# The first six items of a chunked-attention and MLP kernel: one written order of single operations for four engines

## The chip, the cores and the metric

The kernel runs on one core of one Trainium2 chip. The metric is the device time of the whole kernel in microseconds, from one execution to the next; a profile of one execution shows where it goes. Engines are named as the profile names them: PE (TensorE), DVE (VectorE), ACT (ScalarE), POOL (GpSimd), SP (SyncE, which only issues DMAs here).

## What is computed

Attention in chunks of 32 queries, each over 16 keys to the left, its own 32, 8 to the right and 8 memory keys, and behind it two layers of MLP on all 3072 tokens:

```python
# q, k, v: (4, 8, 768, 64); mem_k, mem_v: (4, 8, 8, 64)
for c in range(24):
    k_full = concat(mem_k, k[l_start:r_end])
    scores = scale * matmul(q_c, k_full.T)
    a = exp(scores - max(scores))
    a = a / (sum(a) + 1e-9)
    out[c] = matmul(a, v_full)
x = out as (3072, 512)
h = x @ w_in                       # 512 -> 2048
x = maximum(0.01 * h, h) @ w_out   # 2048 -> 512
return ((x @ w_a) * (x @ w_b)) @ w_out2
```

Matrix products are made with three matmuls each: an operand is split into a rounded high part and a low part that is the rest (xh and xl of the activations, `w[:, 0]` and `w[:, 1]` of a weight, gh and gl of a hidden block).

## The kernel before

**Attention** goes by units of 128 tokens (24 units). For a unit u the kernel loads q, two tiles of keys and two of values, and then goes through these steps: `a_scores(u)` (L273), 32 small matmuls on PE; `a_max(u)` (L293), the maximum of a row and its subtraction on VectorE; `a_exp(u)` (L306), the exponential on ScalarE; `a_soft2(u)` (L325), sum, reciprocal and product on VectorE; `a_turn_mm` (L358), four transposes on PE, and `a_turn_copy` (L369), two copies on ScalarE; `a_pv` (L381), 32 matmuls with the values on PE; `a_out` (L421), the high part on ScalarE and the low part on VectorE. For units in `by_scalar` (L291: 2 and 3) VectorE only negates the maximum, and ScalarE makes eight exponentials of a row each, which subtract and sum at once.

**The first MLP layer** goes by blocks of 512 tokens and by items f of 128 hidden columns. `mm1_pe` (L521) makes a hidden product h_f (12 matmuls), `mm1_act` (L528) its activation g, high part gh (ScalarE) and low part gl (VectorE), `mm2` (L546) the product a_f with the second weight into four accumulators. In block 0 the items 0 to 2 are half items, of the first 256 tokens alone (units 0 and 1); from item 3 on an item needs units 0 to 3.

**Weights** (`class Weights`, L131) arrive as raw 64-bit words, 512 KB a block, in the order h0, h1, h2, a0, h3, a1, h4, a2, ... (numbers 0, 1, 2, ...). A block goes through five steps: `w_bias` on ScalarE (L102), two joins on VectorE (L115, L118), a cast on ScalarE and a low part on VectorE (`cast`, `low`). `step()` (L190) takes one block a step further, twice an item. Blocks of a second weight are also written back to DRAM (`wod`) for later token blocks.

**The order.** `InOrder` (L33) wraps PE, VectorE, ScalarE and SP: as long as it is on, each engine issues in the order in which the code calls it. It is on from the first load through the lines at L458 to L511 and `first_items()` (L611), which ends it. From item 3 on (L987) the order is the scheduler's. `fill(n)` (L471) issues n idle products of the identity with itself on PE (two matmuls each in the trace). Twelve fills stand in the beginning, in two calls.

Buffers that tie steps: four key tiles and four value tiles (two units), two score banks, two p tiles, four raw buffers for the blocks of second weights, three z tiles, two PT tiles, so unit u+2's keys wait until unit u's scores have read theirs, and its values until unit u's product with values has.

Of the kernel before, what the change touches and what calls it, by code (L numbers as in the profile page):

```python
# [55 lines left out]
def kernel(  # L56
# [51 lines left out]
    def w_join(raw, z, part=None):  # L108
        lo, hi = raw[:, :, 0], raw[:, :, 1]
        if part != 1:  # L110
            w_join_hi(hi, z)
        if part != 0:
            w_join_lo(lo, z)
# [17 lines left out]
    class Weights:  # L131
# [7 lines left out]
        def load(self, upto):  # L139
            while self.loaded < min(upto, len(self.order)):  # L140
                f, i = self.order[self.loaded]
                if i:
                    raw = prep.tile([P, 512, 2], I32, tag="raw", name="raw", bufs=4)
                else:
                    raw = wp.tile([P, 512, 2], I32, tag=f"wi{f}", name="raw")
                sp.dma_start(
                    out=raw.rearrange("p n w -> p (n w)"), in_=w1_l[f, i].bitcast(I32)
                )
                self.raw[self.loaded] = raw
                self.loaded += 1  # L150

# [5 lines left out]
        def join(self, part=None):  # L157
            n = self.joined
            if part != 1:
                self.bias(n + 1)  # L160
                self.z[n] = tp.tile([P, 512], I32, tag="z", name="z", bufs=3)
            w_join(self.raw[n], self.z[n], part)
            if part != 0:
                self.raw.pop(n)
                self.joined += 1

        def cast(self, upto):
            while self.casted < min(upto, self.joined):
                n = self.casted
                f, i = self.order[n]  # L170
                pool, tag = (wop, "wo") if i else (wp, f"wi{f}")
                w = pool.tile([P, 2, 512], F32R, tag=tag, name="w")
                act.copy(w[:, 0, :], self.z[n].bitcast(F32))
                wslot[f, i] = w
                self.casted += 1

        def low(self, upto):
            self.cast(upto)
            while self.parted < min(upto, self.joined):
                f, i = self.order[self.parted]  # L180
                w = wslot[f, i]
                dve.tensor_tensor(
                    out=w[:, 1, :], in0=self.z.pop(self.parted).bitcast(F32),
                    in1=w[:, 0, :].bitcast(F32), op=ALU.subtract,
                )
                if i:
                    sp.dma_start(out=wod[f], in_=w.bitcast(F32))
                self.parted += 1

# [101 lines left out]
    by_scalar = (2, 3)  # L291

    def a_max(u):  # L293
        s = st[u]
        m = sm.tile([P, 8], F32, tag="m", name="m", bufs=2)
        dve.reduce_max(m, s, axis=AX.X)
        p = ap_.tile([P, 8, 64], F32, tag="p", name="p", bufs=2)
        if u in by_scalar:
            dve.tensor_scalar(m, m, -scale, None, ALU.mult)
        else:  # L300
            dve.tensor_tensor(
                out=p, in0=s, in1=m.unsqueeze(2).to_broadcast([P, 8, 64]), op=ALU.subtract
            )
        pt_[u] = p, m

    def a_exp(u):  # L306
        s = st.pop(u)
        p, m = pt_[u]
        if u in by_scalar:
            l = sm.tile([P, 8], F32, tag="l", name="l", bufs=2)  # L310
            for r in range(8):
                act.activation(
                    p[:, r], s[:, r], AF.Exp, bias=m[:, r:r + 1], scale=scale,
                    accum_out=l[:, r:r + 1],
                )
            sums[u] = l
        else:
            act.activation(p, p, AF.Exp, scale=scale)
        pt_[u] = p

    def a_soft1(u):
        a_max(u)
        a_exp(u)

    def a_soft2(u):  # L325
# [5 lines left out]
        if u in sums:  # L331
            l = sums.pop(u)
        else:
            l = sm.tile([P, 8], F32, tag="l", name="l", bufs=2)
            dve.reduce_sum(l, p, axis=AX.X)
# [247 lines left out]
    HALF, LEAD = TB // 2, 3  # L583
    items = []
# [25 lines left out]

    def first_items():  # L611
        parts = [items[f][2] for f in range(LEAD)]
        W1.join()
        a_soft2(2)
        h0 = mm1_pe(0, parts[0])
        g0 = mm1_act(*h0)
        W1.bias(4)
        W1.cast(3)
        W1.bias(5)
        a_scores(3)  # L620
        a_max(3)
        W1.low(3)
        a_turn_mm(2, ps_a, "a")
        a_turn_copy(2)
        a_exp(3)
        h1 = mm1_pe(0, parts[1])
        a_pv(2, ps_s, "s")
        W1.join()
        W1.join(0)
        a_soft2(3)  # L630
        W1.join(1)
        W1.cast(4)
        W1.low(4)
        a_out(2, ("x", 0), 2 * UT)
        load_qk(2)
        W1.load(12)
        load_v(2)
        W1.load(13)
        g1 = mm1_act(*h1)
        h2 = mm1_pe(0, parts[2])  # L640
        a_turn_mm(3, ps_s, "s")
        mm2(0, parts[0], g0)
        a_turn_copy(3)
        W1.cast(5)
        W1.bias(6)
        W1.low(5)
        a_pv(3, ps_s, "s")
        W1.join(0)
        a_out(3, ("x", 0), 3 * UT)
        W1.join(1)  # L650
        W1.bias(7)
        g2_low = mm1_act(*h2, low=False)
        W1.cast(6)
        W1.join(0)
        W1.low(6)
        W1.join(1)
        g2 = g2_low()
        W1.cast(7)
        W1.bias(8)
        load_qk(3)  # L660
        load_v(3)
        W1.low(7)
# [324 lines left out]
    for bi, f, parts in items[LEAD:]:  # L987
# [640 lines left out]
```

## Time and profile before

| | us |
|---|---|
| median of 3 runs (lowest, highest) | 1120.43 (1120.24, 1121.39) |
| the profiled execution, own time | 1120.36 |
| its span, first to last instruction | 1118.5 |
| PE busy in the span | 1096.0 (98%) |
| VectorE busy | 772.9 (69%) |
| ScalarE busy | 526.6 (47%) |

The share of busy time tells which engine is the bound over the whole; an idle stretch is found in the 40 slices and in the list of waits, and what stands before and behind it in the timeline. All times below are counted from the start of the span. Matmuls are pipelined: a row's duration overlaps the next, and the distance between starts is what PE takes. Names in the rows are those of the program: s scores, p probabilities, pT and pt the turned ones, pv the product with values, warm the fills, raw, z and w the weight's steps, h, g, gh, gl and a as above. In the first 41 us most lines are L49, the one where `InOrder` issues.

### The profile page before, as it was taken

The numbers are of one execution on the slowest core, as the hardware profiler recorded it, in microseconds if no ns is written. First come the engines' busy times: TensorE is split into PE (matmuls) and PEld (weight loads), VectorE is DVE, ScalarE is ACT, GpSimd is POOL, SyncE is SP. The second block draws the span as 40 slices with busy tenths as digits, with TensorE's granted clock in tenths as the row PEclk, the third lists the DMA queues.
The fourth block names the chain that finished last, engine by engine and source line by source line (L and its number), as shares of the span: only waits on it lengthen the run. The fifth ranks groups of instructions, "written<-read, shape, count | busy, mean of one in ns | idle before, by whom it ended". The sixth has DMA issues, their size and how long they took to land.

```text
span 1118.5 us, 16332 instructions
## 1 busy us (share of the span) xinstructions
PE 1096.0 (98%) x6195; PEld 908.6 (81%) x6195; DVE 772.9 (69%) x1417; ACT 526.6 (47%) x893; POOL 7.4 (1%) x18
## 2 busy tenths in 40 slices
PE   7899999999999999999999999999999999999997
PEld 6788888888888888877788888888888888888886
DVE  6796388978898665778551737588736578745676
ACT  5887556664555235666622424144434243433232
POOL 2000000000000000000000000000000000000000
PEclk9999999999999999999999999999999999999999
DMA  9996889889998423556688756566877566767452
GB/s 315 404 345 229 282 308 344 297 337 365 327 325 335 158 81 135 186 200 226 246 329 290 266 191 201 181 211 193 275 229 219 166 220 192 242 182 242 143 185 76
DMA packets 99854, 270.63 MB, mean 242 GB/s; under 512 B 9664, under 2 KB 24128, under 8 KB 99008
## 3 DMA queue, kind: packets, MB, share of 16 engines
q1 hardware_dynamic: 98032, 267.88, 70.4%
q10 hardware_dynamic: 1744, 1.70, 0.5%
q8 instruction: 49, 0.80, 0.3%
q14 instruction: 29, 0.24, 0.1%
HBM read 215.02 MB, written 54.53 MB: 241 GB/s over the span
## 4 chain that ended last, share of the span: by engine, by line
PE 81%; DVE 9%; ACT 5%; DMA 3%; issue 1%; SPq 1%; DVEq 0%; ACTq 0%
PE ca L49 18%; PE cc L49 9%; PE oa L49 9%; PE a L49 7%; PE cb L49 5%; PE oy L49 4%; PE h L438 4%; PE a L562 4%; PE a L566 3%; PE a L565 3%; PE h L439 3%; PE h L440 3%; DVE pt L351 2%; PE A L49 2%; PE oz L49 1%; PE pv L391 1%
## 5 line engine op out<-in xcount | busy, mean ns | idle before, releaser
L49 PE MATMUL ca<-ch,wab 128*128 128x512 f32 x576 | 192.2, 389 | 0.0
L49 ACT CAST st<-gb 128x512 fp32r<-128x512 f32 x126 | 76.5, 621 | 124.5 <-DVE gb L49 123.9
L49 PEld LDWEIGHTS ca<-ch,wab 128*128 128x128 f32 x576 | 108.1, 188 | 23.2 <-ACT a L49 0.4
L49 PE MATMUL ca<-cl,wab 128*128 128x512 f32 x288 | 112.2, 389 | 0.0
L49 PE MATMUL oa<-st,wt 128*128 128x512 f32 x420 | 104.3, 389 | 0.0
L438 PE MATMUL h<-xh,w 128*128 128x512 f32 (+1 forms) x256 | 100.5, 393 | 2.8 <-DVE xl L425 2.1
L49 PE MATMUL cc<-ch,wab 128*128 128x512 f32 x288 | 100.3, 389 | 0.0
L439 PE MATMUL h<-xl,w 128*128 128x512 f32 (+1 forms) x256 | 98.6, 385 | 0.2 <-DVE xl L49 0.2
L440 PE MATMUL h<-xh,w 128*128 128x512 f32 (+1 forms) x256 | 98.5, 385 | 0.0
L562 PE MATMUL a<-gh,w 128*128 128x512 f32 (+1 forms) x256 | 97.7, 382 | 0.5 <-ACT x L580 0.5
L565 PE MATMUL a<-gl,w 128*128 128x512 f32 (+1 forms) x256 | 97.5, 381 | 0.0
L566 PE MATMUL a<-gh,w 128*128 128x512 f32 (+1 forms) x256 | 97.5, 381 | 0.0
L49 DVE TENSOR_TENSOR st<-gb,st 128x512 fp32r<-128x512 f32 x126 | 85.3, 689 | 15.0 <-ACT st L49 13.3
L49 PEld LDWEIGHTS oa<-st,wt 128*128 128x128 f32 x420 | 78.8, 188 | 16.4
L49 ACT COPY u<-ca 128x512 f32<-128x512 f32 x72 | 42.3, 587 | 91.5 <-PE ca L49 91.4
L351 DVE STREAM_TRANSPOSE pt<-p 32x128 f32<-32x128 f32 x256 | 77.4, 302 | 3.5
L49 PEld LDWEIGHTS cc<-ch,wab 128*128 128x128 f32 x288 | 54.1, 188 | 11.3
L49 PEld LDWEIGHTS ca<-cl,wab 128*128 128x128 f32 x288 | 54.1, 188 | 11.1
L530 ACT ACTIVATE g<-h 128x512 f32<-128x512 f32 (+1 forms) x64 | 37.3, 583 | 54.2 <-PE h L440 53.9
L536 DVE TENSOR_TENSOR gl<-g,gh 128x512 fp32r<-128x512 f32 (+1 forms) x64 | 43.0, 672 | 26.8 <-ACT gh L533 23.2
L438 PEld LDWEIGHTS h<-xh,w 128*128 128x128 f32 x256 | 48.1, 188 | 13.3 <-DVE xl L425 2.5
L562 PEld LDWEIGHTS a<-gh,w 128*128 128x128 f32 x256 | 48.1, 188 | 10.3 <-ACT x L580 0.9
(198 smaller groups left out, 2050.7 us busy)
## 6 DMA issues: line engine op xcount, KB each, us to landing
wab<-wab SPq DMA_DIRECT2D x126, 512.0 KB, 4.4
w<-wod SPq DMA_DIRECT2D x80, 512.0 KB, 5.3
raw<-w SPq DMA_DIRECT2D x68, 512.0 KB, 7.0
wt<-wtd SPq DMA_DIRECT2D x63, 512.0 KB, 4.5
k<-kl SPq DMA_DIRECT2D x48, 256.0 KB, 4.8
v<-vl SPq DMA_DIRECT2D x48, 256.0 KB, 5.6
wab<-pwb SPq DMA_DIRECT2D x12, 768.0 KB, 5.5
wod<-w SPq DMA_DIRECT2D x16, 512.0 KB, 6.8
```

Source lines behind the costliest of these rows:

```text
L49: self.last = emit(*args, **kwargs).ins
L351: dve.transpose(out=pt[o0:o0 + 32, :, 2 * cpar + hpar, hpx, :], in_=p[i0:i0 + 32, hpx::2, 32 * b:32 * b + 32],)
L391: pe.matmul(o[64 * hpar:64 * hpar + 64, 2 * pair:2 * pair + 2, t0:t0 + CH], v[:, i:i + 64], pt[:, 2 * cp + pair, 2 * cpar + hpar].rearrang ...
L438: pe.matmul(ps, w[1], x[0], start=first, stop=False)
L439: pe.matmul(ps, w[0], x[1], start=False, stop=False)
L440: pe.matmul(ps, w[0], x[0], start=False, stop=last)
L530: act.activation(g[:, c], ps[:, c], AF.Prelu, alpha=0.01)
L536: dve.tensor_tensor(out=gl[:, c], in0=g[:, c], in1=gh[:, c].bitcast(F32), op=ALU.subtract)
L562: pe.matmul(ps, slot[:, 1, c], gh[:, t], start=f == 0 and o == 0, stop=False, **kw)
L565: pe.matmul(ps, slot[:, 0, c], gl[:, t], start=False, stop=False, **kw)
L566: pe.matmul(ps, slot[:, 0, c], gh[:, t], start=False, stop=f == NF1 - 1 or (o == HALF and f == LEAD - 1), **kw)
```

## The change

The single steps are made callable one by one (`a_sub`, `a_neg`, `a_sum`, `a_inv`, `a_mult`, `load_one`, `cast_one`, `low_one`, `store`, the two joins), and one string, `FIRST`, lists them in the order in which they are called, for all four engines. It covers the items 0 to 5: in it a word is an operation with its number (s scores, m maximum, d subtraction, n negation, e exponential, S sum, l reciprocal, p product, T turn, ca and cb its copies, O product with values, xh and xl the parts of the output, b, zh, zl, c, w the weight's steps, h, g, gh, gl, a the item's, Qa and Qb the halves of a unit's placement, F fills, q, k, v, raw, id, st DMAs).

- Keys of unit 2 and 3 and their queries are loaded ahead of values and of most weights; weight blocks come in the order 1, 2, 0, 3, 4, 12, 5, 14, 6, 9, 8, 7, 13, ...
- The second half of q and the second key tile of units 0 and 1 are issued by ScalarE's queue.
- The scores of units 0 to 3 come before the first product with values; the score of unit 4, its maximum, subtraction and exponential come within the list.
- Unit 3 leaves `by_scalar`: its subtraction and sum move to VectorE.
- Fills: 8, 5, 11 and 10 in place of 6 and 6.
- The turn of unit 3 and the products with values of units 2 and 3 use the bank pool of the accumulators.
- The fixed order ends behind item 5 (`FIXED = 6`) with 12 weight blocks done and 16 loaded; before it ended with item 2. From item 6 on the scheduler orders as before.

```diff
             if u < len(qs):
-                eng = act if u < 1 else sp
+                eng = act if u < 2 else sp
...
             t = ap_.tile([P, 512], F32, tag="k", name="k")
-            sp.dma_start(out=t, in_=ku[u][cp])
+            (act if u < 2 and cp else sp).dma_start(out=t, in_=ku[u][cp])
...
-    by_scalar = (2, 3)
+    by_scalar = (2,)
...
+    def a_sub(u):
+        p, m = pt_[u]
+        dve.tensor_tensor(
+            out=p, in0=st.pop(u), in1=m.unsqueeze(2).to_broadcast([P, 8, 64]), op=ALU.subtract
+        )
+
+    def a_neg(u):
+        m = pt_[u][1]
+        dve.tensor_scalar(m, m, -scale, None, ALU.mult)
...
-    q_load(1)
-    k_load(2)
-    q_load(2)
-    k_load(4)
-    sp.dma_start(out=ident, in_=id_l)
-    W1.load(1)
-    v_load(2)
-    W1.load(2)
-    q_load(3)
...
-    a_scores(0)
-    a_scores(1)
-    fill(6)
-    k_load(6)
-    v_load(4)
-    W1.load(3)
-    q_load(4)
-    k_load(8)
-    W1.load(5)
-    a_max(0)
-    a_exp(0)
-    W1.bias(1)
-    a_soft2(0)
-    a_turn_mm(0, ps_a, "a")
-    fill(6)
-    a_max(1)
-    a_turn_copy(0, (0,))
-    a_exp(1)
-    a_turn_copy(0, (1,))
-    W1.bias(2)
-    a_pv(0, ps_h, "h")
-    v_load(6)
-    W1.load(7)
-    W1.join(0)
-    a_soft2(1)
-    W1.join(1)
-    a_out(0, ("x", 0), 0)
-    a_turn_mm(1, ps_a, "a")
-    a_scores(2)
-    a_turn_copy(1)
-    W1.join()
-    W1.cast(2)
-    W1.low(1)
-    a_max(2)
-    a_pv(1, ps_h, "h")
-    v_load(8)
-    W1.load(11)
-    a_out(1, ("x", 0), UT)
-    W1.bias(3)
-    W1.low(2)
-    a_exp(2)
...
+    FIXED, DONE = 6, 12
...
+    FIRST = """
+        q0 k0 q1 k1 s0 q2 k2 m0 d0 s1 e0 raw1 S0 m1 s2 id l0 q3 k3 d1 p0 e1 m2 b1 T0 F8 n2 raw2
+        S1 e2 zh1 zl1 s3 v0 l1 p1 ca0 l2 cb0 raw0 T1 p2 c1 m3 T2 F5 b2 v1 d3 cb1 O0 F11 zh2 e3
+        raw3 w1 ca1 zl2 xh0 v2 S3 b0 l3 ca2 raw4 O1 F10 xl0 c2 zh0 cb2 v3 zl0 xh1 p3 c0 raw12
+        xl1 T3 b3 O2 w0 ca3 raw5 w2 h0 b4 zh3 cb3 raw14 zh4 xh2 O3 zl4 g0 raw6 zl3 gh0 h1 c4 xl2
+        raw9 xh3 w4 h2 b5 xl3 raw8 g1 zh5 c3 h3 gl0 g2 raw7 zl5 b6 w3 gh1 c5 zh6 q4 raw13 zl6 b9
+        a0 k4 w5 c6 gl1 b8 k5 w6 a1 b7 zh8 gh2 zl8 Qb4 h4 zh9 raw10 zh7 Qa4 zl7 raw15 gl2 c7 s4
+        c8 w7 raw11 g3 zl9 a2 w8 v4 c9 gh3 m4 h5 v5 b10 d4 w9 e4 st0 b11 gl3 g4 zh10 a3 st1 zh11
+        g5 zl11 st2 zl10 c11 w11 c10 gh5 w10 q5 st3 gh4 gl5 gl4 st4
+    """
...
+        op("q", lambda u: q_load(u + 1))
+        op("k", lambda u: k_load(2 * u + 2))
+        op("v", lambda u: v_load(2 * u + 2))
+        op("id", lambda n: sp.dma_start(out=ident, in_=id_l))
+        op("raw", W1.load_one)
+        op("st", lambda f: W1.store(f))
+        op("s", a_scores)
+        op("m", a_max)
+        op("d", a_sub)
+        op("n", a_neg)
+        op("e", a_exp)
+        op("S", a_sum)
+        op("l", a_inv)
+        op("p", a_mult)
+        op("T", a_turn_mm, ps_a, "a")
+        op("ca", a_turn_copy, (0,))
+        op("cb", a_turn_copy, (1,))
+        op("O", lambda u: a_pv(u, *((ps_h, "h") if u < 2 else (ps_a, "a"))))
+        op("xh", out_hi)
+        op("xl", out_lo)
+        op("b", lambda n: w_bias(W1.raw[n]))
+        op("zh", zh)
+        op("zl", zl)
+        op("c", W1.cast_one)
+        op("w", W1.low_one)
+        for name, fn in (("h", h), ("g", g), ("gh", gh), ("gl", gl), ("a", a)):
+            op(name, fn)
+        op("Qa", q_place_half, 0)
+        op("Qb", q_place_half, 1)
+        op("F", fill)
+        for word in FIRST.split():
+            name = word.rstrip("0123456789")
+            ops[name](int(word[len(name):] or 0))
+        qr.pop(4)
+        W1.loaded = 16
+        W1.biased = W1.joined = W1.casted = W1.parted = DONE
+        load_qk(4)
         for e in (pe, dve, act, sp):
             e.on = False
-        return [(0, parts[1], g1), (0, parts[2], g2)]
-
-    at(0, 3, q_place, 4, nc.scalar.copy)
+        return [(0, items[f][2], made.pop(f)) for f in (FIXED - 2, FIXED - 1)]
...
     for k, f in enumerate([5, 8, 11, 14]):
         u = TB // UT + k
-        at(0, f, a_scores, u)
-        at(0, f, load_qk, u)
-        at(0, f, a_soft1, u)
+        if k:
+            at(0, f, a_scores, u)
+            at(0, f, load_qk, u)
+            at(0, f, a_soft1, u)
...
-    for bi, f, parts in items[LEAD:]:
+    for bi, f, parts in items[FIXED:]:
```

## Rows read from the trace of the kernel before

**Rows 1.** The page, parts 1 and 2: PE's share of the span, and 40 slices.
```profile
PE 1096.0 (98%) x6195; PEld 908.6 (81%) x6195; DVE 772.9 (69%) x1417; ACT 526.6 (47%) x893; POOL 7.4 (1%) x18
...
PE   7899999999999999999999999999999999999997
```

**Rows 2.** PE's waits, whole span: waiting <- releaser: us, times, longest.
```profile
PE s L46 <- DMA k<-kl: 6.1, 1, 6.1
PE h L438 <- DVE xl L425: 2.1, 3, 0.9
```

**Rows 3.** PE's timeline: start us, us, instruction, count; idle time and releaser.
```profile
8.56 2.04 PE L49 MATMUL s<-k,qs 128*64 128x64 f32 x32 [0.39 <-DMA k<-kl]
...
12.63 0.60 PE L49 MATMUL pT<-id,p 128*128 128x128 f32 x4
13.06 1.50 PE L49 MATMUL warm<-id 128*128 128x128 f32 x12
...
16.90 2.00 PE L49 MATMUL s<-k,qs 128*64 128x64 f32 x32
18.74 1.10 PE L49 MATMUL pv<-pt,v 128*64 128x64 f32 x32
...
26.91 1.15 PE L49 MATMUL pv<-pt,v 128*64 128x64 f32 x32
27.99 0.39 PE L49 MATMUL h<-xh,w 128*128 128x256 f32 x1
...
38.58 0.28 PE L562 MATMUL a<-gh,w 128*128 128x256 f32 x1
...
38.93 0.28 PE L562 MATMUL a<-gh,w 128*128 128x256 f32 x1
...
52.28 0.50 PE L438 MATMUL h<-xh,w 128*128 128x512 f32 x1
...
55.14 0.39 PE L562 MATMUL a<-gh,w 128*128 128x512 f32 x1
...
57.86 0.39 PE L438 MATMUL h<-xh,w 128*128 128x512 f32 x1
```

**Rows 4.** The chain of waits, 0 to 120 us: start us, us, what.
```profile
3.90 4.53 DMA k<-kl
...
21.04 2.37 ACT p L49 x16
...
70.50 0.93 PE s L282 x32
```

**Rows 5.** Stretches: length, busy us by engine, granted clock, DMA share, GB/s.
```profile
0.00:5.00 5.00, 0.00 (x0) 0.00 (x0) 0.97 (x2) 1.28 (x1) 4.25 (x12) 1.00 0.42 122
...
10.00:20.00 10.00, 9.24 (x140) 8.52 (x136) 8.70 (x18) 6.37 (x12) 0.00 (x0) 1.00 1.05 343
20.00:30.00 10.00, 8.69 (x104) 7.81 (x104) 7.33 (x19) 9.93 (x43) 0.00 (x0) 1.00 1.04 401
...
8.20:52.30 44.10, 38.88 (x417) 33.71 (x417) 36.33 (x72) 35.10 (x86) 0.00 (x0) 1.00 1.03 386
```

**Rows 6.** ScalarE's timeline: its wait for the first weight block.
```profile
11.52 0.69 ACT L49 ACTIVATE raw<-raw 128x512 f32<-128x512 f32 x1 [1.22 <-DMA raw<-w]
```

**Rows 7.** VectorE by shape, 0 to 52.3 us: count, busy us, mean ns, idle before.
```profile
L49 DVE TENSOR_TENSOR w<-z,w 128x512 fp32r<-128x512 f32 x7 | 4.8, 690 | 1.7 <-ACT w L49 1.7
...
L116 DVE TENSOR_SCALAR z<-raw 128x512 int32<-128x512 int32 x6 | 2.4, 421 | 0.0
```

**Rows 8.** ScalarE by shape, 0 to 52.3 us.
```profile
L49 ACT ACTIVATE raw<-raw 128x512 f32<-128x512 f32 x8 | 5.4, 681 | 1.2 <-DMA raw<-w 1.2
...
L49 ACT ACTIVATE p<-p 128x512 f32<-128x512 f32 x2 | 1.3, 630 | 7.0 <-DVE p L49 7.0
```

**Rows 9.** Two stretches, the fills alone (x is the count of matmuls).
```profile
10.50:11.75 1.25, 1.22 (x5) 1.22 (x6) 1.00 1.01 365
13.05:14.30 1.25, 1.24 (x12) 1.25 (x12) 1.00 1.02 267
```

More of the change, by code (lines that the diff above doesn't have):

```diff
@@ L106, in w_bias, with w_join @@
         act.activation(hi, hi, AF.Prelu, scale=2.0 ** -112, alpha=2.0 ** 32)
[L108 to L113, printed above, removed]
+    def w_join(raw, z):
+        w_join_hi(raw[:, :, 1], z)
+        w_join_lo(raw[:, :, 0], z)
     def w_join_hi(hi, z):
@@ L140, in load, with load_one @@
             while self.loaded < min(upto, len(self.order)):
[L141 to L149, printed above, removed]
-                self.loaded += 1
+                self.load_one(self.loaded)
+                self.loaded += 1
+        def load_one(self, n):
+            f, i = self.order[n]
+            if i:
+                raw = prep.tile([P, 512, 2], I32, tag="raw", name="raw", bufs=4)
+            else:
+                raw = wp.tile([P, 512, 2], I32, tag=f"wi{f}", name="raw")
+            sp.dma_start(
+                out=raw.rearrange("p n w -> p (n w)"), in_=w1_l[f, i].bitcast(I32)
+            )
+            self.raw[n] = raw
         def bias(self, upto):
@@ L179, in low, with low_one, store @@
             while self.parted < min(upto, self.joined):
+                self.low_one(self.parted)
                 f, i = self.order[self.parted]
[L181 to L185, printed above, removed]
                 if i:
-                    sp.dma_start(out=wod[f], in_=w.bitcast(F32))
+                    self.store(f)
                 self.parted += 1
+        def low_one(self, n):
+            w = wslot[self.order[n]]
+            dve.tensor_tensor(
+                out=w[:, 1, :], in0=self.z.pop(n).bitcast(F32),
+                in1=w[:, 0, :].bitcast(F32), op=ALU.subtract,
+            )
+        def store(self, f):
+            sp.dma_start(out=wod[f], in_=wslot[f, 1].bitcast(F32))
         def step(self):
@@ L290, with a_exp, a_sum @@
     pt_, sums = {}, {}
-    by_scalar = (2, 3)
+    by_scalar = (2,)
     def a_max(u):
-        s = st[u]
         m = sm.tile([P, 8], F32, tag="m", name="m", bufs=2)
[L296 to L302, printed above, removed]
-            )
[L304 to L319, printed above, removed]
+        dve.reduce_max(m, st[u], axis=AX.X)
+        pt_[u] = ap_.tile([P, 8, 64], F32, tag="p", name="p", bufs=2), m
+    def a_sub(u):
+        p, m = pt_[u]
+        dve.tensor_tensor(
+            out=p, in0=st.pop(u), in1=m.unsqueeze(2).to_broadcast([P, 8, 64]), op=ALU.subtract
+        )
+    def a_neg(u):
+        m = pt_[u][1]
+        dve.tensor_scalar(m, m, -scale, None, ALU.mult)
+    def a_exp(u):
+        p, m = pt_[u]
+        pt_[u] = p
+        if u not in by_scalar:
+            act.activation(p, p, AF.Exp, scale=scale)
+            return
+        s = st.pop(u)
+        l = sums[u] = sm.tile([P, 8], F32, tag="l", name="l", bufs=2)
+        for r in range(8):
+            act.activation(
+                p[:, r], s[:, r], AF.Exp, bias=m[:, r:r + 1], scale=scale,
+                accum_out=l[:, r:r + 1],
+            )
     def a_soft1(u):
         a_max(u)
+        a_sub(u)
         a_exp(u)
-    def a_soft2(u):
+    def a_sum(u):
         p = pt_[u]
@@ L330, in a_soft2, with a_inv, a_mult @@
             dve.memset(p[64:128, 4:8, WIN - RIGHT:WIN], 0.0)
[L331 to L335, printed above, removed]
+        l = sums[u] = sm.tile([P, 8], F32, tag="l", name="l", bufs=2)
+        dve.reduce_sum(l, p, axis=AX.X)
+    def a_inv(u):
+        l = sums[u]
         dve.tensor_scalar(l, l, 1e-9, None, ALU.add)
         dve.reciprocal(l, l)
+    def a_mult(u):
+        p, l = pt_[u], sums.pop(u)
         dve.tensor_tensor(
@@ L340, in a_soft2 @@
         )
+    def a_soft2(u):
+        a_sum(u)
+        a_inv(u)
+        a_mult(u)
     def a_turn(u):
@@ L609, in load_v @@
         v_load(2 * u + 6)
-    def first_items():
[L612 to L662, printed above, removed]
@@ new lines, with q_place_half, zh, zl @@
+    """
+    def first_items():
+        made, ops = {}, {}
+        def q_place_half(u, h):
+            t = qr[u].rearrange("p q o -> p o q")
+            d = slice(64 * h, 64 * h + 64)
+            act.copy(q_tile(u)[d, :, CH * h:CH * h + CH], t[d])
+        def zh(n):
+            W1.z[n] = tp.tile([P, 512], I32, tag="z", name="z", bufs=3)
+            w_join_hi(W1.raw[n][:, :, 1], W1.z[n])
+        def zl(n):
+            w_join_lo(W1.raw.pop(n)[:, :, 0], W1.z[n])
+        def h(f):
+            made[f] = mm1_pe(0, items[f][2])
+        def g(f):
+            ps, c = made[f]
+            t = tp.tile([P, TB], F32, tag="t", name="g")
+            act.activation(t[:, c], ps[:, c], AF.Prelu, alpha=0.01)
+            made[f] = t, c
+        def gh(f):
+            t, c = made[f]
+            x = tp.tile([P, TB], F32R, tag="gh", name="gh", bufs=3)
+            act.copy(x[:, c], t[:, c])
+            made[f] = t, c, x
+        def gl(f):
+            t, c, x = made[f]
+            y = tp.tile([P, TB], F32R, tag="gl", name="gl", bufs=3)
+            dve.tensor_tensor(
+                out=y[:, c], in0=t[:, c], in1=x[:, c].bitcast(F32), op=ALU.subtract
+            )
+            made[f] = x, y
+        def a(f):
+            mm2(0, items[f][2], made.pop(f))
+        def out_hi(u):
+            act.copy(x1["x", 0][0][:, :, u * UT:u * UT + UT], pvt[u])
+        def out_lo(u):
+            hi, lo = [t[:, :, u * UT:u * UT + UT] for t in x1["x", 0]]
+            dve.tensor_tensor(out=lo, in0=pvt.pop(u), in1=hi.bitcast(F32), op=ALU.subtract)
+        def op(name, fn, *args):
+            ops[name] = lambda n: fn(n, *args)
+        op("q", lambda u: q_load(u + 1))
[35 more added lines that the diff above has]
+        load_qk(4)
```

27 lines of the change are left out of this document (13 added, 14 removed).

## Prediction

> **What bounds the kernel now.** I read the page first: PE is busy 98% of the span, and the digits of its row are 9 from the second slice on [rows 1]. So an order of work can pay only at the beginning. The list of PE's waits says the same: the largest is the 6.1 us before the first scores, and of the later ones only the 2.1 us ahead of L438 stand out [rows 2]. Then PE's timeline: the rows to look at are the start of item 6's first product at 52.28 us and those behind it, at 55.14 and 57.86, which follow without a gap [rows 3]. From 52.28 us on PE simply works; whatever the change gives must be there by then. At that point the kernel of before has done, on PE, the hidden products h0 to h5, the output products a0 to a3, units 0 to 3 and the scores of unit 4. The fixed list of the change ends with exactly the same PE work. So the forecast is one question: **when does the changed kernel reach h6?** Each us there is a us at the end, as far as the later work follows PE, which its gapless rows say.
>
> **What PE must do in the list, piece by piece** [rows 3, 4]. Scores of a unit from the strided tiles: 16.90 to 18.74, 1.84 us. Scores of unit 4: 0.93. A turn (four transposes): 12.63 to 13.06, 0.44. A product with values: 26.91 to 27.99, 1.08. Half items: three matmuls of 256 columns take 38.58 to 38.93, so twelve take 1.43. Full items: 55.14 to 57.86, 2.73. A fill is two matmuls of 128 columns: twelve take 1.50 us with the tail of the last, and the four transposes of the same size 0.11 each; I take 0.111, so 0.223 for a fill.
> The change has F8, F5, F11 and F10: 34 fills, 7.6 us, against 12 (2.7 us) now. They stand in PE's queue and can't be skipped; this is the cost that is added on the path. What it can remove is PE's idle and stretched time: over 8.2 to 52.3 us PE is busy 38.88 of 44.10 us, fills included [rows 5].
>
> **Loads.** Their order sets when PE's list begins in earnest. Now the queue carries q0, k0, q1, k1 (1.57 MB), the identity, a weight block (2.16 MB), values, another weight block, and only then k2 and, after more of the same, k3. The first weight block has landed at 11.52 us, where ScalarE's wait for it ends [rows 6]; from there the DMA engines are full (share 1.05) and move 343 GB/s until 20 us and 401 GB/s after it [rows 5]. With keys ahead of values, k2 is complete at 2.36 MB, the identity at 2.95 and k3 at 3.74: 11.52 + 0.20/0.343 = 12.1 us, 13.8 us, and 11.52 + 1.57/0.343 = 16.1 us. Unit 2's scores now begin at 16.90 [rows 3] and could begin almost 5 us earlier.
> The ACT queue takes halves of q0, q1, k0 and k1. Before 5 us the DMA engines are used at 0.42 [rows 5], and SP reaches the key block of unit 1 only at 3.90 us, which then takes until 8.43 [rows 4]. Issuing four of eight loads elsewhere can move the stream forward by 0 to 1.1 us; I take 0, since k2 must still wait until unit 0's scores have read k0's buffers, and keep 1.1 for the early end. The Trainium skill ("DMA: Bandwidth & Descriptors", section "Issuing engines are not separate DMA queues") speaks against a gain here: starting DMAs from several engines saves only the time of starting them. By it the sum stays as it is; the low share before 5 us says that the starting does cost something in this stretch.
> The weights pay for it: the block that a2 needs becomes the last of 11.6 MB. At these rates it lands at 36.3 us; a2 comes at 43.2 us below. Its five steps (ScalarE 0.68, VectorE 0.42 and 0.69, ScalarE 0.63, VectorE 0.69) take 3.1 us [rows 7, 8], so 3.8 us are left for queueing. Off the path.
>
> **The sum.** T0 waits for the identity, 13.8 us. (Unit 0's softmax is earlier: its turn starts at 12.63 now [rows 3], and one more VectorE operation of 0.69 stands ahead of its last step that unit 0's exponential doesn't cover: 13.3.) Then in PE's order: T0 0.44 and F8 1.78 end at 16.0; k3 is there at 16.1. From there s3 1.84, T1 and T2 0.88, F5 1.11, O0 1.08, F11 2.45, O1 1.08, F10 2.23 (26.8 us); T3 0.44, O2 1.08, h0 1.43, O3 1.08, h1 and h2 2.86, h3 2.73, a0 and a1 2.86, h4 2.73, s4 0.93, a2 1.43, h5 2.73, a3 2.73: **h6 at 49.8 us** if nothing waits. The values of units 0 and 1 (4.78 and 5.83 MB: 19.2 and 21.9 us) are there before O0 (19.9) and O1 (23.6).
>
> **Who else could be late.** VectorE now works 36.33 us between 8.2 and 52.3 and idles 7.8 [rows 5]. Up to the block that h6 needs the list has four large operations more (unit 4's maximum and subtraction are earlier, unit 3 subtracts and sums on VectorE), one small one less, one weight block less and two large gl less: 4 x 0.69 - 0.17 - 1.80 - 1.38 = -0.6, so 35.7 us. That block is ready at 8.2 + 35.7 = 43.9 us plus VectorE's idle time: 5.9 us of it are free, and with the 7.8 us of now h6 would start at 51.7. ScalarE loses work: eight exponentials with sums of unit 3, 2.37 us [rows 4], become one of 0.63 [rows 8]; it is 35.10 of 44.10 us busy [rows 5] and not the bound. The methods split into single operations issue the same instructions and cost nothing; half of unit 4's placement and its exponential only move on ScalarE.
>
> **The clock.** The column of the granted clock reads 1.00, that is 2.4 GHz, from the start [rows 5], but from 10.50 us on five fill matmuls and six weight loads go in 1.25 us (0.21 each by the loads), from 13.05 on twelve of both [rows 9]: the full rate shows only after PE had worked from 6.1 us with no pause over 0.39 us [rows 2, 3]. In the list PE pauses between s1 (ends about 10) and s2 (about 12). If the full rate comes only at the end of F8, T0 and F8 take 0.87 + 16 x 0.21 and s3 starts at 18.1 instead of 16.1: h6 at 51.8. No row shows the case, so these are the two ends, 49.8 and 51.8. I take the middle, 50.8, since the pause is short and F8 alone is longer than the 1.2 us of fills before the rise now, and add 0.2 for handovers: **h6 at 51.0, 1.3 us ahead of 52.28.** The Trainium skill ("TensorE: Matmul & The Clock Gate", "Part 1: The HAM clock gate") says that the array starts at the lower rate and that the moment of the rise changes from run to run; by it neither end is ruled out, and the doubled number of fills agrees with such a rise.
>
> **Rivals.** (1) *Early.* The second queue brings the stream up to 1.1 us forward and the rate rises before F8: s3 starts at 15.0 to 15.9, h6 at 48.8 to 49.8, a gain of 2.5 to 3.5 us, 1116.9 to 1117.9. For it: DMA engines half idle before 5 us. Against: k2 waits for unit 0's scores, and VectorE may then idle under 5.9 us. (2) *VectorE becomes the bound:* it idles as much as now, h6 at 51.7, 1119.8; with one us more of it 1120.8. For it: twelve weight blocks go to and fro between ScalarE and VectorE in a fixed order, where one late operand holds all behind it. Against: four softmaxes that come earlier fill its early gaps. (3) *The clock, slower than before.* If the rate stays low past F8, the price beside the 2.0 us is 0.9 for T1 and T2, 1.1 for F5, 2.4 for F11 and 2.2 for F10. It makes the kernel slower by over 2.2 us (h6 past 54.5) from a rise at about 26 us on, in F11; low through F10 gives h6 at 58.4, 1126.5. For it: PE's pause before s2. Against: by then PE would have worked without a pause for 14 us. (4) *SP's queue stands.* The third unit's values wait for O0 and the fourth's for O1, and behind them in SP's order are five weight blocks that a1, h4, a2, h5 and a3 need. O1 ends at 24.6; a load took 4.5 us (3.90 to 8.43) [rows 4], so the stream may pause 2 us and a2's block land at 38.3, within its 3.8 us. If O1 ends 4 us later than summed, a2 waits, 1120.5 to 1123.
>
> **How the numbers follow.** The profiled execution took 1120.36 us, 1.86 more than its span of 1118.5; the median of the runs is 1120.43, so I work from 1120.36. Forecast 1120.36 - 1.3 = 1119.1 us, chance 0.50, its own range 1118.2 to 1120.5. Rival 1: 0.28. Rival 2: 0.08. Rival 3: 0.07. Rival 4: 0.07, of which 0.03 lie above the bound. A measurement of this kernel tells about 0.2%, 2.2 us, from no change. So faster 0.28, same 0.50 + 0.08 + 0.04 = 0.62, slower 0.07 + 0.03 = 0.10. The range goes from 1117.0 (rival 1 all but whole) to 1121.8 (rival 4's middle); rival 3 is left out.
>
> **What would show it.** Right: s3 at 16 to 18 us, T3 at 27 to 29, h6's first row of L438 at 50 to 52, no PE wait over 0.5 us between s2 and h6. Six fill loads to 1.25 us after 17 us would show the slow rate; VectorE idle for over 6 us with h6 waiting for a weight block rival 2; s3 before 15.9 rival 1; ScalarE waiting for a weight's DMA after 30 us rival 4. The forecast is wrong if T3 comes after 29.5, or if PE has new waits behind h6: the order there is free as before and may be laid differently, up to 1 us around L438's waits.

## The result, and the profile after

| | us, median (lowest to highest) |
|---|---|
| before | 1120.34 (1118.74 to 1121.39), 4 runs |
| after | 1132.97 (1131.77 to 1134.67), 4 runs |
| ratio | 1.0115, 95% interval 1.0101 to 1.0128 |

The change makes the kernel 12.6 us slower; 1.3 us faster was forecast, and the range ended at 1121.8. The profiled execution of after took 1134.67 us with a span of 1132.9, 14.4 more than the span of before, so its rows hold some 2 us more than the median does. Lines of after's code are moved against before's: its L454 is L438 of before, L441 is L425, L526 is L562, L544 is L580, L378 is L362 and L389 is L373.

The page of after, parts 1 and 2; the rows answer to [rows 1]:

```profile
PE 1103.7 (97%) x6239; PEld 915.8 (81%) x6239; DVE 773.0 (68%) x1418; ACT 523.9 (46%) x878; POOL 7.4 (1%) x18
...
PE   6999999999999999999999999999999999999997
```

The slices show one digit that differs, the first. PE is busy 7.7 us longer and still 97% of the span: nothing here points to 14 us. The list of PE's waits does (after, whole span: waiting <- releaser: us, times, longest), beside [rows 2]:

```profile
PE s L46 <- DMA k<-kl: 6.6, 1, 6.6
PE a L526 <- ACT x L544: 4.6, 4, 2.4
PE h L454 <- DVE xl L441: 3.8, 3, 2.3
PE a L526 <- ACT gh L49: 2.7, 1, 2.7
PE pT L49 <- DVE l L49: 1.9, 1, 1.9
```

The 6.6 stands at the very start (6.1 before). Two lie in the stretch of the list or at its end (the 1.9 and the 2.7). The 4.6 and the 3.8 come far behind it, in token blocks that the change doesn't touch.

**The list's beginning.** PE's timeline of after (start us, us, instruction, count; idle time and releaser):

```profile
15.23 0.63 PE L49 MATMUL pT<-id,p 128*128 128x128 f32 x4 [1.88 <-DVE l L49]
15.70 3.08 PE L49 MATMUL warm<-id 128*128 128x128 f32 x16
18.71 2.00 PE L49 MATMUL s<-k,qs 128*64 128x64 f32 x32
```

T0 comes at 15.23, F8 takes 3.08 us in place of 1.78, and s3 starts at 18.71, not at 16.1. The stretches below (length, then busy us of PE, its loads, DVE, ACT, POOL; granted clock, DMA share, GB/s) show why F8 is long: the clock was granted at 0.50, 1.2 GHz, for 3.4 us.

```profile
16.30:19.70 3.40, 3.40 (x31) 3.17 (x30) 2.37 (x7) 3.35 (x18) 0.00 (x0) 0.50 1.03 410
57.20:60.60 3.40, 3.40 (x8) 2.65 (x9) 3.40 (x8) 1.59 (x3) 0.00 (x0) 0.51 1.04 331
248.40:251.60 3.20, 3.15 (x8) 2.48 (x8) 1.80 (x5) 3.17 (x7) 0.00 (x0) 0.50 0.86 314
```

**The list's end.** PE's timeline of after, around h6, which was at 52.28 before [rows 3]:

```profile
53.54 0.39 PE L49 MATMUL a<-gh,w 128*128 128x512 f32 x1
53.77 0.60 PE L378 MATMUL pT<-id,p 128*128 128x128 f32 x4
57.12 0.71 PE L526 MATMUL a<-gh,w 128*128 128x512 f32 x1 [2.75 <-ACT gh L49]
57.63 0.63 PE L454 MATMUL h<-xh,w 128*128 128x512 f32 x1
...
64.31 0.39 PE L454 MATMUL h<-xh,w 128*128 128x512 f32 x1
```

PE is through with the list at 53.77, and h6 is what the prediction had next. In its place come the four transposes of unit 4 (L378), which the code calls behind item 6 and which stood at 63.3 us before; then the first matmul of a4, which waits 2.75 us for gh. ScalarE's timeline says why gh is late:

```profile
51.25 1.07 ACT L49 ACTIVATE g<-h 128x512 f32<-128x512 f32 x2
54.41 0.58 ACT L389 COPY pt<-pT 64x512 f32<-64x512 f32 x1 [2.08 <-PE pT L378]
54.89 1.14 ACT L49 CAST w<-z 128x512 fp32r<-128x512 f32 x2
55.93 1.14 ACT L49 CAST gh<-g 128x512 fp32r<-128x512 f32 x2
```

and VectorE's shows the rest of unit 4 (L340 to L349, from behind the list), and the list's last two weight blocks (L49):

```profile
50.59 0.68 DVE L340 TENSOR_REDUCE l<-p 128x8 f32<-128x512 f32 x1
51.30 0.17 DVE L344 TENSOR_SCALAR l<-l 128x8 f32<-128x8 f32 x1
51.51 0.20 DVE L345 RECIPROCAL l<-l 128x8 f32<-128x8 f32 x1
51.75 0.69 DVE L349 TENSOR_TENSOR p<-p,l 128x512 f32<-128x512 f32 x1
...
55.54 1.29 DVE L49 TENSOR_TENSOR w<-z,w 128x512 fp32r<-128x512 f32 x2 [0.63 <-ACT w L49]
```

The last operations of the list (L49: c11, c10, gh5, gh4) are behind a copy of unit 4's turn (L389), which isn't in the list. ScalarE stands 2.08 us for PE to reach that turn, and behind it PE stands for the gh that ScalarE then makes. On VectorE the sum and product of unit 4 (L340 to L349) have also gone between operations of the list. But for its last 0.3 us h6 itself could not have come in the gap either: its weight block, number 10, is the second of the two at 55.54 and done at 56.83, since it needs ScalarE's cast c10, late for the same reason. So the list fixes the order of its own operations among themselves; what follows it in the code may still be put among them.

The bill up to h7 (64.31, before 57.86 [rows 3]: 6.45 us): the list ends 1.49 us after the old h6; the wait is 2.75; unit 4's turn and one matmul of a4, moved ahead of h6, take 1.1; and from h6 to h7 it is 6.68 us in place of 5.58, since the clock is at 0.51 from 57.2 to 60.6. Together 6.44. A part of it is work done earlier and comes back: unit 4's turn need not be made behind h7. At h14, in after and then in before, the lag is 5.94:

```profile
107.72 0.48 PE L454 MATMUL h<-xh,w 128*128 128x512 f32 x1
```

```profile
101.78 0.48 PE L438 MATMUL h<-xh,w 128*128 128x512 f32 x1
```

**Far behind the list.** ScalarE's timeline, first of after at 243 us, then of before at the same place of the program, 236 us. L544 (L580 in before) copies a finished token block out of the accumulators that its next product needs; L122 (L125) casts weights of the second layer.

```profile
243.48 0.41 ACT L122 CAST pwa<-pz 128x256 fp32r<-128x256 f32 x1 [4.06 <-DVE pz L116]
245.40 1.04 ACT L122 CAST pwb<-ps 128x1024 fp32r<-128x1024 f32 x1 [1.52 <-DVE ps L795]
246.35 0.59 ACT L494 ACTIVATE g<-h 128x512 f32<-128x512 f32 x1
246.84 0.58 ACT L544 COPY x<-a 128x512 f32<-128x512 f32 x1
```

```profile
236.07 0.58 ACT L580 COPY x<-a 128x512 f32<-128x512 f32 x1
236.54 0.63 ACT L533 CAST gh<-g 128x512 fp32r<-128x512 f32 x1
237.06 1.57 ACT L580 COPY x<-a 128x512 f32<-128x512 f32 x3
238.49 0.45 ACT L125 CAST pwa<-pz 128x256 fp32r<-128x256 f32 x1
```

Before, the copies go first, and the casts of pwa (128x256) and pwb follow them. After, these two casts, which wait 4.06 and 1.52 us for VectorE, stand ahead of the copies, and PE waits for the first copy:

```profile
247.47 0.50 PE L526 MATMUL a<-gh,w 128*128 128x512 f32 x1 [2.35 <-ACT x L544]
```

Then the clock is at 0.50 until 251.6, which is 1.6 us more. Behind h14 these waits come to 4.6 - 0.5 = 4.1 us more for copies and 3.8 - 2.1 = 1.7 more for xl, with [rows 2] and the 0.5 of before's own list of waits; with the clock 7.4 us. 5.94 + 7.4 = 13.3 of the 14.4 us; the rest is not assigned.

So two things have to be told apart: what the list itself is worth (its end is 1.49 us late here), and what the order costs that the scheduler lays around and behind it.

### The profile page after: what moved, and what is told of

It reads as the page before. It is cut to its first block, busy times and chain, and to the rows that moved or that the text cites. A ratio compares the mean times of both kernels' runs of the same rounds, so it can differ in the third digit from the quotient of the medians.

```text
span 1132.9 us, 16415 instructions
## 1 busy us (share of the span) xinstructions
PE 1103.7 (97%) x6239; PEld 915.8 (81%) x6239; DVE 773.0 (68%) x1418; ACT 523.9 (46%) x878; POOL 7.4 (1%) x18
## 4 chain that ended last, share of the span: by engine, by line
PE 85%; DVE 6%; DMA 4%; ACT 3%; issue 1%; SPq 0%; DVEq 0%; ACTq 0%
PE ca L49 18%; PE cc L49 9%; PE a L49 8%; PE oa L49 8%; PE cb L49 5%; PE oy L49 4%; PE a L526 4%; PE h L454 3%; PE a L529 3%; PE a L530 3%; PE h L456 3%; PE h L455 3%; PE A L49 3%; DVE pt L367 2%; PE oz L49 1%; PE C L49 1%
## 5 line engine op out<-in xcount | busy, mean ns | idle before, releaser
L49 PE MATMUL ca<-ch,wab 128*128 128x512 f32 x576 | 192.2, 389 | 0.0
L49 ACT CAST st<-gb 128x512 fp32r<-128x512 f32 x126 | 76.5, 622 | 124.5 <-DVE gb L49 123.9
L49 PEld LDWEIGHTS ca<-ch,wab 128*128 128x128 f32 x576 | 108.1, 188 | 23.1 <-ACT a L49 0.4
L49 PE MATMUL ca<-cl,wab 128*128 128x512 f32 x288 | 112.1, 389 | 0.0
L49 PE MATMUL oa<-st,wt 128*128 128x512 f32 x420 | 104.3, 389 | 0.0
L526 PE MATMUL a<-gh,w 128*128 128x512 f32 (+1 forms) x244 | 95.3, 391 | 7.4 <-ACT x L544 4.6
L49 PE MATMUL cc<-ch,wab 128*128 128x512 f32 x288 | 100.4, 389 | 0.0
L454 PE MATMUL h<-xh,w 128*128 128x512 f32 (+1 forms) x244 | 96.2, 394 | 3.8 <-DVE xl L441 3.8
L49 DVE TENSOR_TENSOR st<-gb,st 128x512 fp32r<-128x512 f32 x126 | 85.3, 688 | 15.1 <-ACT st L49 13.3
L455 PE MATMUL h<-xl,w 128*128 128x512 f32 (+1 forms) x244 | 94.3, 387 | 0.0
L529 PE MATMUL a<-gl,w 128*128 128x512 f32 (+1 forms) x244 | 94.3, 386 | 0.0
L456 PE MATMUL h<-xh,w 128*128 128x512 f32 (+1 forms) x244 | 94.3, 386 | 0.0
L530 PE MATMUL a<-gh,w 128*128 128x512 f32 (+1 forms) x244 | 94.1, 386 | 0.0
L49 PEld LDWEIGHTS oa<-st,wt 128*128 128x128 f32 x420 | 78.8, 188 | 16.4
L49 ACT COPY u<-ca 128x512 f32<-128x512 f32 x72 | 42.3, 587 | 91.5 <-PE ca L49 91.4
L49 PEld LDWEIGHTS cc<-ch,wab 128*128 128x128 f32 x288 | 54.1, 188 | 11.3
L49 PEld LDWEIGHTS ca<-cl,wab 128*128 128x128 f32 x288 | 54.0, 188 | 11.0
L526 PEld LDWEIGHTS a<-gh,w 128*128 128x128 f32 x244 | 46.2, 189 | 18.6 <-ACT x L544 6.6
L454 PEld LDWEIGHTS h<-xh,w 128*128 128x128 f32 x244 | 46.2, 190 | 13.6 <-DVE xl L441 4.2
```

Source lines behind the costliest of these rows:

```text
L49: self.last = emit(*args, **kwargs).ins
L454: pe.matmul(ps, w[1], x[0], start=first, stop=False)
L455: pe.matmul(ps, w[0], x[1], start=False, stop=False)
L456: pe.matmul(ps, w[0], x[0], start=False, stop=last)
L526: pe.matmul(ps, slot[:, 1, c], gh[:, t], start=f == 0 and o == 0, stop=False, **kw)
L529: pe.matmul(ps, slot[:, 0, c], gl[:, t], start=False, stop=False, **kw)
```

## Experiments

All ratios are to the kernel before, run beside it on the same chip, with 95% intervals.

### The order behind the list, crossed with the list

The tie used in several kernels: at the code's item 6 a mark is set, and at the end each engine's later instructions (`mine`) are chained in a recorded order (`places`). It adds an order of issue and no wait. With it the list can run with before's order, and before's beginning with after's order.

```diff
+    for e, places in pinned_order().items():
...
+        for a, b in zip(places, places[1:]):
+            tc.add_manual_dep(
+                mine[b], mine[a].name,
+                mybir.DependencyInfo(mybir.DependencyClass.NoSync, mybir.DependencyReason.DATA),
+                reason="pinned",
+            )
```

**list_old_order**: the list of the change, and behind it before's order. So that both have the same work behind the mark, three weight steps stand at the list's end:

```diff
         W1.biased = W1.joined = W1.casted = W1.parted = DONE
         load_qk(4)
+        W1.load(24)
+        W1.join()
+        W1.bias(15)
```

> The changed list, with 24 weight blocks issued and a 13th joined right behind it so that everything traced from item 6 on is the same as in the kernel of before, and each engine's order from item 6 on tied to the one that the kernel of before has. Theory O (most of the loss is the order that the scheduler lays behind the list): item 6's product at 53.5 to 55 us, no wait for the output copies of a token block, end 1121 to 1124 us. Theory L (the list itself leaves weights, loads or VectorE behind, and PE pays later whatever the order): 1128 to 1134 us, with the waits for output copies of 2 us still there.

Measured: 1121.05 us, ratio 1.0008 (0.9998 to 1.0017). That is 1.05 us above the 1120.00 of before beside it, so of the 12.6 us some 11.6 are gone, with the list as it was. The tie does what it should: behind 80 us the instructions of PE, VectorE and ScalarE stand in before's order, one for one. The waits for output copies are gone too, those for xl are at 2.1 as before, and nothing stands ahead of h6 but a wait for a weight block:

```profile
14.86 0.63 PE L49 MATMUL pT<-id,p 128*128 128x128 f32 x4 [1.47 <-DMA id<-eye]
...
28.43 0.60 PE L49 MATMUL pT<-id,p 128*128 128x128 f32 x4
...
53.12 0.50 PE L454 MATMUL h<-xh,w 128*128 128x512 f32 x1 [0.69 <-DVE w L49]
```

**list_state**, the control: the same three weight steps, the order free.

> The changed list with the same extra steps behind it (24 blocks issued, a 13th joined), but the order from item 6 on left to the scheduler. Theory O: the scheduler still lays another order, so 1128 to 1135 us, as the changed kernel. A third theory S (the list stops one block short and that is what is missing later): 1121 to 1125 us.

Measured: 1133.42 us, 1.0122 (1.0104 to 1.0140); the waits are after's, 3.2 us for output copies, 3.4 for xl and 2.7 ahead of h6. The steps are not what helps. Behind 80 us PE's order is before's here too, one for one, and so it is in after: what the scheduler laid differently there is the order on ScalarE (641 of 767 instructions in the same sequence) and on VectorE.

**old_list_new_order**: before's beginning, untouched, and behind it the order that the scheduler laid in list_state.

> The kernel of before up to item 5, with each engine's order from item 6 on tied to the one that the scheduler lays behind the changed list (of the kernel with the extra steps). Theory O: slower than before by 5 to 11 us, 1125 to 1131, with waits of PE for output copies between 130 and 360 us. Theory L: 1119 to 1122.

Measured: 1133.51 us, 1.0128 (1.0111 to 1.0145). Not one operation of the list is in it, and it is as slow as after, and slower than the expected 1125 to 1131. Its waits (PE, whole span):

```profile
PE pT L362 <- DVE p L338: 4.8, 1, 4.8
PE a L562 <- ACT x L580: 3.2, 3, 2.1
PE h L438 <- DVE xl L425: 2.9, 3, 1.6
```

The first is unit 4's turn, again put ahead of item 6, where unit 4 is not ready; ahead of h6 the equal times therefore rest on different waits (4.8 here, 2.7 in list_state). By the four corners (1120.0 for before, 1121.05, 1133.5, 1133.4) the order is worth 12.4 to 13.5 us, and the list 0 to 1. **The loss is the order behind the list.**

**list_old_order_block0**: list_old_order with the tie on the first token block alone. It asks whether there are two places.

```diff
+        if (bi, f) == (1, 0):
+            mark.append(nc.cur_bb.bb.instructions[-1].name)
...
+    upto = [i.name for i in traced].index(mark[1])
+    tied = {i.name for i in traced[:upto]}
...
+        places = [x for x in places if mine[x].name in tied]
```

> The changed list as in list_old_order, but the order of before is tied on each engine only for the work of the first token block's items; from the second block on the scheduler lays it freely. It tells whether the loss has one place or two. Two places (unit 4's turn ahead of h6 at 54 us, and the order from the second block on): h6 at 53.1 as in list_old_order, no PE pause of 2 us near 55, but again PE waits of 2 to 5 us in sum at output products for ScalarE's copies of the output and for xl, and a total between the two, 1121 + 6 to 9 = 1127 to 1130 us. One place, the early turn with what follows from it: 1121 us, and no such waits. If all of it lies behind the first block: 1133 us.

Measured: 1127.01 us, 1.0064 (1.0050 to 1.0078), h6 at 52.68. So there are two places: with the first block held some 6.0 us are still lost (from 1121.05), and 6.4 are not (to 1133.4). These two are no prices of the places, since the order behind the first block is another one here: list_state lies 3.3 us behind before at h14 and 8.5 more at the last item, this kernel 0.4 and 5.0 more. In one point the expectation missed: the waits are partly others.

```profile
PE h L454 <- DVE xl L441: 2.9, 3, 1.7
PE pv L407 <- ACT g L494: 1.8, 2, 1.1
...
PE a L529 <- DVE gl L500: 0.8, 1, 0.8
PE a L526 <- ACT x L544: 0.5, 1, 0.5
```

Here PE waits 1.8 us for products with values behind ScalarE's activations, and for the copies no longer than before. The scheduler has laid a third order, and it too loses some 6 us, elsewhere. PE's own order is before's again; it is ScalarE's and VectorE's that differ. It is therefore not one wrong pair of operations that costs the second part.

### Parts of the change, each alone

**unit3_alone**: before, with unit 3 taken from ScalarE's sums, the order free.

```diff
-    by_scalar = (2, 3)
+    by_scalar = (2,)
```

> One part of the change alone: unit 3 leaves by_scalar, nothing else. VectorE +1.2 us, ScalarE -1.7 us of work before 35 us. Theory O: that alone lets the scheduler lay another order behind it, so the time moves by more than these: 1122 to 1130. Theory L: within 1 us of before, 1119.5 to 1121.5.

Measured: 1124.51 us, 1.0041 (1.0026 to 1.0056). h6 is at 53.26, 1.0 us late; the rest stands far behind, in waits that before has shorter (2.1 for xl) or not at all:

```profile
PE h L438 <- DVE xl L425: 4.3, 3, 1.9
PE pv L391 <- ACT g L530: 2.8, 2, 2.3
```

**unit3_old_order**: the same with before's order tied behind item 5.

> Unit 3 leaves by_scalar, as in unit3_alone, but each engine's order from item 6 on is tied to that of the kernel of before. Theory O (order): the 4.5 us that unit3_alone lost are gone, 1119.5 to 1121.5 us. If moving the subtraction and sum to VectorE costs by itself: 1123 to 1125.

Measured: 1120.64 us, 1.0006 (0.9994 to 1.0019). The edit itself costs nothing that can be told; the order that the scheduler makes of it costs some 4 us. It is the same finding in small: one line in the beginning, and 4 us at 150 to 350 us.

**second_queue_alone**: before, with the halves of unit 1's keys and queries issued by ScalarE's queue, as in the change's first two edits.

> Before, with the halves of unit 1's queries and keys issued by ScalarE's queue as in the change, and nothing else. The prediction took this edit at 0 with an early end of 1.1 us. By the first: 1120.1 us within 0.5, and unit 1's second key block lands at 8.4 to 9.1 us as before. By the early end: unit 1's scores up to 1.1 us earlier and a total of 1119.0.

Measured: 1120.20 us, 0.9996 (0.9985 to 1.0007). Nothing, as the prediction took it.

### The list itself: identity and fills

The four kernels here are list_old_order with words of the string moved or left out.

**list_id_early**: the identity's load right behind the keys of unit 1.

```diff
-        q0 k0 q1 k1 s0 q2 k2 m0 d0 s1 e0 raw1 S0 m1 s2 id l0 q3 k3 d1 p0 e1 m2 b1 T0 F8 n2 raw2
+        q0 k0 q1 k1 id s0 q2 k2 m0 d0 s1 e0 raw1 S0 m1 s2 l0 q3 k3 d1 p0 e1 m2 b1 T0 F8 n2 raw2
```

> list_old_order with one word moved: the identity is loaded right behind the keys of unit 1, ahead of unit 2's, so that the first turn needn't wait for it (it waited until 14.86 us, 1.5 us of PE idle). Theory P (PE's own list, fills included, is the path to item 6): T0 at about 13.9, h6 0.7 to 1.0 us earlier, 1119.8 to 1120.5 us. Theory V (VectorE and the weights are the path, h6 waited 0.7 us for one): h6 where it was, 53.1 us, and 1120.5 to 1121.5.

Measured: 1121.03 us, 1.0008 (0.9996 to 1.0021), as without it. T0 starts at 13.77, 1.1 us earlier, and h6 at 53.14, no earlier: PE waits 1.00 us there for VectorE's weight block, in place of 0.69. An earlier T0 isn't what h6 waits for.

**list_no_fill**: the identity where the change has it, and none of the 34 fills.

> list_old_order without any of its 34 fills (7.9 us of PE). Theory P: they are on the path as far as VectorE lets PE go: h6 at 50 to 51.5 us, 1118 to 1119.5 us, the clock stays high. Theory C (the fills hold the clock): PE pauses, the granted clock falls and the half items take up to twice as long, h6 at 53 to 56, 1121 to 1124. Theory V: h6 unchanged at about 53, 1120.5 to 1121.5.

Measured: 1119.10 us, 0.9984 (0.9973 to 0.9996), h6 at 53.06. 8.1 us of fills are gone from PE's queue, and h6 is where it was in the profiled execution (1120.13 us, 1.0 over the median): T0 waits 2.27 us for the identity, and PE, with pauses of 2.27, 1.09 and 2.15 us, works at a low clock (the third figure from the right below: 0.82 of full speed from 16 to 24 us, 0.61 from 24 to 32).

```profile
16.00:24.00 8.00, 5.66 (x99) 4.66 (x99) 6.52 (x15) 7.28 (x25) 0.00 (x0) 0.82 0.98 366
24.00:32.00 8.00, 5.86 (x63) 5.27 (x58) 7.00 (x14) 5.87 (x11) 0.00 (x0) 0.61 0.97 375
```

None of the three theories holds whole: h6 and the clock are as theory C has them, the time is theory P's.

**list_id_11_fills**: the identity early, and 4, 2, 3 and 2 fills in place of 8, 5, 11 and 10.

> list_old_order with the identity early and 11 fills (4, 2, 3, 2) in place of 34. Theory P: h6 at 49 to 51 us, 1117 to 1119 us, faster than both kernels. Theory V: h6 at 52.5 to 53, 1120 to 1121. Theory C: a fallen clock in the list, h6 at 52 to 55.

Measured: 1117.66 us, 0.9974 (0.9964 to 0.9985): 2.4 us faster than before, and the fastest kernel here. The clock stays at 1.00, T3 is at 24.67, h6 at 50.26 (a stretch of it, then PE's row of h6):

```profile
24.00:32.00 8.00, 7.33 (x105) 6.92 (x106) 6.80 (x13) 7.35 (x15) 0.00 (x0) 1.00 0.99 374
```

```profile
50.26 0.50 PE L454 MATMUL h<-xh,w 128*128 128x512 f32 x1 [1.48 <-DVE w L49]
```

**list_id_no_fill**: the identity early and no fills.

> list_id_11_fills without its eleven fills: the list, before's order tied behind it, the identity early. If a few fills pay for themselves because the granted clock falls in the pauses that they close (list_no_fill showed 0.79 to 0.87 between 10 and 40 us): clock under 0.9 between 10 and 40 us, h6 at 52 to 53 and 1118.5 to 1119.5 us, over 1 us above list_id_11_fills. If PE's pauses alone counted and the fills were only in the way: clock 1.00, h6 at 50 or earlier, 1117.7 us or less.

Measured: 1118.83 us, 0.9992 (0.9980 to 1.0003). The clock is low between 16 and 24 us alone (0.79), and h6 comes at 50.45, again after 1.50 us of waiting for VectorE's weight block. The expected h6 of 52 to 53 was wrong. Whether eleven fills are worth having is not settled: h6 differs by 0.2 us, and the two intervals overlap.

What the four show together: with 34 fills the identity's place is worth nothing; without fills it is worth 2.6 us at h6 (53.06 to 50.45) in one profiled execution of each, and nothing that the medians show (ratios 0.9984 and 0.9992). So h6 is not the whole time. In the two kernels with h6 near 50 PE stands 1.5 us ahead of h6 for VectorE, so VectorE sets the end of the list, and what lets it finish sooner is that it stands less. Here are both kernels over the stretch of [rows 5] (fourth figure: VectorE's busy time of 44.10 us), first list_old_order, then list_id_11_fills:

```profile
8.20:52.30 44.10, 42.01 (x470) 38.05 (x467) 35.80 (x71) 33.96 (x72) 0.00 (x0) 1.00 0.98 349
```

```profile
8.20:52.30 44.10, 38.88 (x425) 34.21 (x424) 38.52 (x76) 34.80 (x74) 0.00 (x0) 1.00 1.01 379
```

VectorE idles 8.3 us with 34 fills and 5.6 with 11; up to each kernel's own h6 it is the same (8.30 of 44.90 us, 5.58 of 42.00). Half of these 2.7 us less is a wait for work that stands behind PE's fills: in list_old_order ScalarE waits 1.3 us for products with values, 1.0 of it for O1, which has F11 right ahead of it, before it can make xh, and VectorE waits 1.3 us for that xh. Both waits are there in list_id_early too, which has the 34 fills, and neither is left in list_id_11_fills. The other half are waits for ScalarE's casts and exponentials, and what shortened those is not shown. The fills were put in PE's queue as PE's cost; through O1 they are VectorE's too.

## Why the prediction was wrong, point by point

- **The step that failed: "Each us there is a us at the end, as far as the later work follows PE".** The whole sum was made for h6, and the free order behind it was priced in the last paragraph at "up to 1 us around L438's waits". The order behind the list costs 12.4 us or more (list_old_order against list_state, and old_list_new_order against before). PE's gapless rows behind h6 [rows 3] showed that before's order feeds PE; they say nothing of another order, and the change gave the scheduler another beginning to plan from. Not even PE's order had to change for it: behind 80 us that is before's in after, and what PE waits for is laid differently on ScalarE and VectorE. Of before's 98% [rows 1] I read that the later work can't get better; that it can get worse was in the same figure.
- **No rival held it.** The rivals on the slower side were the clock (3) and SP's queue (4). Two of the forecast's own signs of being wrong did come, T3 at 29.93 (the limit was 29.5) and new waits behind h6. The clock does fall in after, but in F8 for 3.4 us and then behind two of the later waits. Clock and waits together are the loss; the cause of the waits is the order.
- **The list's own gain, 1.3 us, was not there: 53.1 in place of 51.0 at h6, in list_old_order.** Three terms, 3.3 us in all, of which the 1.2 added for the clock and handovers cover a part. T0: 14.86 in place of 13.8, since the identity lands later than worked out. The rate between 10 and 20 us is 327 GB/s, where 343 was used; over the 2.3 us for which it was used that is 0.1 us. The rest goes back to the premise that the loads keep the DMA engines full: in list_old_order SP waits for unit 0's scores and a key load, issues unit 2's keys at 7.88 us and the identity at 9.63 (before: 5.00), and that lands 5.1 us later; between 5 and 15 us 266 GB/s move, in before 330. The prediction named k2's wait for the scores and let the loads run on. T0 to T3: 13.6 us in place of 13.0, from fills of 8.1 us (1.88, 1.21, 2.65, 2.34 from start to start) for 7.6. From T3 to h6: 24.7 us in place of 23.0, of it 0.69 of waiting for VectorE's block; the rest is handovers, for which the sum had 0.2. (Two slips in the sum bear on nothing: by its own terms O1 comes at 23.5, not 23.6, and a2 at 42.9, not 43.2.) Rival 2 is nearest to what happened at h6, where an earlier T0 brought nothing (list_id_early): it gave 51.7 with 7.8 us of VectorE's idle time, VectorE idles 8.3, and 1120.8 for one us more stands against 1121.05. Its chance of 0.08 was too low: the sum had 5.9 us of idle time free for VectorE, and a product that stands behind fills uses up 1.3 of them.
- **The clock: the place, F8, was rightly named and the price lay between the ends; the pause was another, and to that extent it was luck.** The prediction feared the pause between s1 and s2. In after these two run on without one (PE's row at 9.60, 64 matmuls in 3.76 us), and the pause is the 1.88 us ahead of T0. F8 is at 1.2 GHz from 16.3 on and costs 1.1 us (3.08 for 1.95 in list_old_order); there, after a pause of 1.47 us, it isn't. So the price of 2.0 us was an upper end.
- **The parts priced at nothing were worth nothing:** unit 3 (1.0006, 0.9994 to 1.0019) and the second queue (0.9996, 0.9985 to 1.0007). For the queue the run agrees with the Trainium skill ("DMA: Bandwidth & Descriptors", "Issuing engines are not separate DMA queues"), by which starting DMAs from several engines saves only the time of starting them. But only with the order held is unit 3 worth nothing; left to the scheduler it costs 4.5 us (1124.51 against 1120.0).
- **Loads and SP's queue (rival 4):** ScalarE's waits for a weight's load are 2.4 us in five between 8 and 52 us in after, none over 0.9, where the rival needed a pause of 2 us and more. Its sign, such a wait after 30 us, did come (0.5 us at 34 and at 42), but not its size, and PE's list shows no wait for a weight's load.

**Open.** Why the scheduler lays unit 4's turn ahead of h6, and the casts ahead of the copies, was not tried: its own reckoning of times isn't in a trace. What the runs show is that three orders which it laid (for the change, for unit 3 alone, and from the second block on) were all worse than before's, by 4 to 13 us.

## What to carry to other kernels

A change to the beginning of a kernel whose rest is ordered by a scheduler changes the rest: price that rest as an unknown of its own, from the tightest waits of all that lies behind and on every engine, or tie it before the edit is judged. A list that is fixed among its own operations doesn't keep later work out, so put what must not come between into it, or end it where an intruder would wait for nothing. And idle products on the busiest engine are not only that engine's cost: ask whose operands stand behind them.

## What the runs showed of the hardware

That pauses of some 2 us can cost the clock was not in the sum. The granted clock read 0.50 to 0.53, 1.2 GHz, for 3.2 to 3.6 us after single pauses of PE: of 2.75 us (57.2 to 60.6 in after), 2.35 us (248.4 to 251.6 in after), 4.83 us (56.8 to 60.4 in old_list_new_order) and 1.88 us (16.3 to 19.7 in after). After others it did not fall: 1.47 us ahead of T0 in list_old_order, 1.99 us at 24.3 in list_id_no_fill, and 2.30 us at 327.6 in after. In list_state two of the pauses of after stand again at the same places of the program and with the same lengths, 1.88 us ahead of T0 and 2.75 ahead of h6, and the clock stays at 1.00 behind both. So the length of the pause alone does not decide it, and what else does is open; where it fell, the wait cost 1.1 us (F8) to some 1.6 us (the products behind 57.2 and 248.4 in after) more than its length.
